# Another list of places for scores and values, and two more load and result tiles for the weight conversion, in an attention-and-MLP kernel

## The chip, the cores and the metric

The kernel is one program on one core of a Trainium2 chip. The metric is the time of one execution on the device in microseconds (us). The time before is the median of three runs. One more execution was taken with the hardware profiler; every duration below comes from that one, and its own time is given beside its span.

A core has five engines that run their own instruction lists in order and wait for each other by semaphores: PE (matrix multiply, with its weight loads shown apart as PEld), DVE (vector), ACT (activation and copies), POOL (a second vector engine) and SP (which only issues transfers here). Matrix results land in PSUM, a small memory of banks of 128 x 512 floats; DVE and ACT move them to the main on-chip memory.

## The reference, cut to what matters

```python
def _attn_ref(q, k, v, w_pre, w_post):            # q, k, v: (8, 12, 448, 64)
    scores = scale * np.matmul(q, k.transpose(0, 1, 3, 2))
    scores = np.einsum('bhij,hg->bgij', scores, w_pre)      # mix the 12 heads
    scores = scores - np.max(scores, axis=-1, keepdims=True)
    attn = np.exp(scores)
    attn = attn / (np.sum(attn, axis=-1, keepdims=True) + 1e-09)
    attn = np.einsum('bhij,hg->bgij', attn, w_post)          # mix them again
    return np.matmul(attn, v)

def _moe_ref(x, w_in, w_out):                      # x: (3584, 768)
    h = x @ w_in                                   # w_in: (768, 2048)
    g = h - np.tanh(h)
    return g @ w_out                               # w_out: (2048, 768)
```

The attention result of all 8 batches, put in token order, is x of the second function. w_in and w_out arrive as 64-bit floats.

## The kernel before, in words

The program has two stages. The first, to about 850 us of the profiled span, is the attention; the second is the MLP, and the change does not touch it. While the attention runs, the two weight matrices are also converted, from 64-bit floats to pairs of 32-bit parts (a high part and a rest), and written to device memory for the second stage.

**Blocks, groups, places.** A batch of 448 query rows is cut into four blocks of 120, 120, 120 and 88 rows; there are 32 blocks. The 12 heads are handled as six pairs. Since the heads are mixed with each other, the scores of a block are first computed for all heads and put in a tile `s` (rows by heads by 448 keys); then groups of 10 query rows x 12 heads are gathered from it by a transfer into a tile `t` with one partition for each row and head, so that mixing heads is a matrix product. A block has 12 such groups (the short one 9), 360 in all. The main loop handles two groups at a time, and one turn of it is called a **place**: there are 180, numbered from 0. In place p the loop issues, in this order:

- the gathers of the two groups that are used two places later, and up to six transfers that wait in two lists (lines 510 and 369, on SP);
- `premix`: four products with `w_pre` on PE (line 521), which give the mixed scores of the two groups, in two PSUM banks;
- `norm` for the place before: one over the sums on DVE (lines 541, 542) and the scaled `w_post`, called `wr`, on POOL (line 543);
- `expo`: two row maxima on DVE (line 530) and two exponentials on ACT (line 532);
- the jobs listed for this place: `prep_k` (transposing two heads of keys, line 417), `prep_q` (transposing queries, line 443), `values` (24 products of the finished attention of a block with v, line 602; half a block's heads in one job), `scores` (six products for a head pair, line 477), and loads;
- `sooner`: the copies of these jobs' results, the two copies of a pair's scores being one on ACT and one on DVE (line 482);
- `mix` for the place before: 16 products with `wr` (line 560), into the one tile `ps_o`; it waits for `wr`, and for `ps_o` to have been copied out;
- `conv.place()`: some steps of the weight conversion;
- at the start of the next place, the copy of `ps_o` into the block's tile `at` on ACT (line 570, or line 577 twice where the two groups are of different blocks).

Every engine runs its instructions in exactly this order (a final pass pins it), so a late instruction holds all behind it on its engine.

**The list of places.** Which place does which job is worked out when the program is built. Before, `scores` jobs come two head pairs at a time: three entries for a block, each with an earliest place and a due place; one entry (two pairs of scores, or one `values` job) is handed to each place by due place, and after an entry of one kind the other kind goes first where there is time. Scores of a block are due three places before the place in which the block's first group is used. A place may get nothing at all.

**The conversion.** `narrow_steps` deals with 56 chunks of 128 x 512 (w_in, 24 chunks) or 128 x 384 (w_out, 32 chunks) numbers. A chunk is loaded (`cr`), goes through 11 steps (`narrow_chunk`; DVE lines 80, 83, 87, 89, 94; ACT lines 82, 85, 102; POOL lines 96, 98, 104, in the order 80, 82 and 83, 85, 87, 89, 94, 96, 98, 102, 104), and its two results are written (`ws<-cs`, `ws<-cl`). At most two chunks are active, and their steps are taken in turn, one of each; 617 steps are spread over 164 places from place 4 on, so 3.76 a place. A loaded chunk becomes active when one of the two is done and its load was issued at least one place ago; three chunks are loaded or active at most. The load list is only served behind the attention's own transfers.

## Time and profile before

| what | value |
|---|---|
| median of 3 runs (lowest to highest) | 1794.49 us (1794.04 to 1794.81) |
| the profiled execution's own time | 1788.92 us |
| its span | 1787.2 us |
| PE, PEld busy in the span | 98%, 80% |
| DVE, ACT, POOL busy in the span | 63%, 56%, 18% |
| mean granted PE clock | 0.993 |
| bytes moved by transfers | 372.32 MB, mean 208 GB/s |

A matmul's end is modelled in this profile, so PE counts as busy nearly always; that does not say that it runs at its peak. What is to be read is the idle time in front of a group of instructions, and what ended it. In rows of groups the columns are: line, engine, operation, out<-in, shapes, count | busy us, mean ns of one | idle us before them, and what ended most of it. In rows of the timeline: start us, duration us, engine, line, operation, out<-in, shapes, count, and in brackets the idle time before and what ended it. A matmul that runs as two passes is counted twice.

### The profile page before, as it was taken

Reading aid. Unit: us, or ns where it says so; the run is one execution under the profiler, and the core shown is the slowest. Engines: PE = TensorE matmul, PEld = TensorE weight load, DVE = VectorE, ACT = ScalarE, POOL = GpSimd, SP = SyncE. Lnnn points to the kernel's source line nnn. Section 1 sums busy time; section 2 is a strip of 40 time slices with the busy share of each in tenths; the row PEclk is TensorE's granted clock in tenths of the full one; section 3 lists DMA queues with packets and bytes.
Section 4 is the critical chain, followed back from the end, with each engine's and each line's share of the span. In section 5 each row is a group of like instructions: output and inputs, shape, how many; then the busy total and the mean of one; then the engine's idle time right before and its main releaser. Section 6 shows DMA issues by size and latency. Waiting matters only on the chain.

```text
span 1787.2 us, 41382 instructions
## 1 busy us (share of the span) xinstructions
PE 1751.0 (98%) x16572; PEld 1425.6 (80%) x16572; DVE 1128.3 (63%) x2362; ACT 1000.5 (56%) x2051; POOL 320.1 (18%) x417
## 2 busy tenths in 40 slices
PE   8999999999999999999999999999999999999998
PEld 6777777777777777777888888888888888888887
DVE  5676777777777767664556566565565565655555
ACT  5777877777777776765343443433434434444333
POOL 1333333333333333321010010000000000000000
PEclk9999999999999999999999999999999999999999
DMA  8668687777967687565655655655656655655651
GB/s 176 204 196 216 194 236 224 217 215 215 249 203 218 215 213 220 178 202 216 255 207 194 248 193 207 241 193 214 229 197 216 224 208 204 228 217 190 230 194 36
DMA packets 232816, 372.32 MB, mean 208 GB/s; under 512 B 98992, under 2 KB 207536, under 8 KB 218288
## 3 DMA queue, kind: packets, MB, share of 16 engines
q1 hardware_dynamic: 231740, 368.45, 64.0%
q8 instruction: 131, 2.15, 0.5%
q10 hardware_dynamic: 884, 1.22, 0.2%
q14 instruction: 61, 0.50, 0.1%
HBM read 245.37 MB, written 47.19 MB: 164 GB/s over the span
## 4 chain that ended last, share of the span: by engine, by line
PE 87%; DMA 4%; ACT 4%; DVE 3%; issue 1%; POOL 0%; SPq 0%; ACTq 0%; DVEq 0%; POOLq 0%
PE ps_o L560 13%; PE ps_h L257 8%; PE ps_h L258 8%; PE ps_h L262 8%; PE ps_m L602 8%; PE ps_p L521 7%; PE ya L305 6%; PE ya L302 6%; PE ya L303 6%; PE ps_q L477 5%; PE yb L305 3%; PE yb L303 3%; PE yb L302 3%; DMA t<-s 2%; PE ps_m L443 1%
## 5 line engine op out<-in xcount | busy, mean ns | idle before, releaser
L560 PEld LDWEIGHTS ps_o<-wr,e 60*112 60x112 f32 (+1 forms) x5760 | 306.2, 176 | 44.3 <-POOL wr L543 21.8
L560 PE MATMUL ps_o<-wr,e 60*112 60x60 f32 (+1 forms) x5760 | 315.5, 259 | 14.3 <-POOL wr L543 7.7
L530 DVE TENSOR_REDUCE mx<-ps_p 128x1 f32<-128x448 f32 x360 | 207.7, 619 | 163.9 <-PE ps_p L521 163.7
L532 ACT ACTIVATE e<-ps_p,mx 128x448 f32<-128x448 f32 x360 | 225.7, 634 | 101.9 <-DVE mx L530 99.4
L289 ACT CAST gh<-r 128x512 fp32r<-128x512 f32 x112 | 69.6, 621 | 372.6 <-DVE r L282 372.6
L258 PE MATMUL ps_h<-xl,w 128*128 128x512 f32 x672 | 264.4, 393 | 0.0
L257 PE MATMUL ps_h<-xh,w 128*128 128x512 f32 x672 | 264.3, 393 | 0.0
L570 ACT COPY at<-ps_o 112x960 f32<-112x960 f32 x156 | 153.7, 985 | 93.8 <-PE ps_o L560 93.2
L247 POOL TENSOR_TENSOR xl<-rx,xh 128x512 fp32r<-128x512 f32 x38 | 55.6, 1464 | 731.2 <-ACT xh L246 731.2
L521 PE MATMUL ps_p<-t,wpre 60*64 60x448 f32 (+1 forms) x1440 | 180.8, 569 | 3.9 <-DMA t<-s 2.7
L305 PE MATMUL ya<-w,gl 128*128 128x512 f32 x448 | 177.0, 395 | 0.7 <-DVE gl L290 0.7
L278 DVE SCALAR_TENSOR_TENSOR r<-qa,ps_h 128x512 f32<-128x512 f32 x112 | 77.1, 688 | 159.2 <-ACT t L275 159.2
L302 PE MATMUL ya<-w,gh 128*128 128x512 f32 x448 | 174.8, 390 | 1.0 <-ACT gh L289 1.0
L303 PE MATMUL ya<-w,gh 128*128 128x512 f32 x448 | 174.8, 390 | 0.0
L602 PEld LDWEIGHTS ps_m<-at,vr 112*64 112x64 f32 x3072 | 147.5, 137 | 31.0 <-ACT at L577 10.9
L262 PE MATMUL ps_h<-xh,w 128*128 128x512 f32 x672 | 170.6, 389 | 0.0
L602 PE MATMUL ps_m<-at,vr 112*64 112x120 f32 (+1 forms) x3072 | 161.6, 261 | 8.4 <-ACT at L577 3.1
L272 ACT ACTIVATE u<-ps_h 128x512 f32<-128x512 f32 x112 | 67.0, 599 | 152.9 <-PE ps_h L262 152.9
L262 PEld LDWEIGHTS ps_h<-xh,w 128*128 128x128 f32 x672 | 126.3, 188 | 26.3
L258 PEld LDWEIGHTS ps_h<-xl,w 128*128 128x128 f32 x672 | 127.5, 190 | 23.7
L257 PEld LDWEIGHTS ps_h<-xh,w 128*128 128x128 f32 x672 | 127.4, 190 | 23.4
L543 POOL TENSOR_TENSOR wr<-wpost,zs 128x120 f32<-128x120 f32 x180 | 70.2, 390 | 402.9 <-DVE zs L542 293.6
(93 smaller groups left out, 3038.0 us busy)
## 6 DMA issues: line engine op xcount, KB each, us to landing
w<-ws SPq DMA_DIRECT2D x112, 1536.0 KB
t<-s SPq DMA_DIRECT2D x342, 210.0 KB
cr<-in_moe_w_in_dram SPq DMA_DIRECT2D x24, 512.0 KB
cr<-in_moe_w_out_dram SPq DMA_DIRECT2D x32, 384.0 KB
vr<-in_v_dram SPq DMA_DIRECT2D x24, 448.0 KB
kr<-in_k_dram SPq DMA_DIRECT2D x23, 448.0 KB
out_dram<-ob SPq DMA_DIRECT2D x24, 384.0 KB
qr<-in_q_dram SPq DMA_DIRECT2D x23, 360.0 KB
```

What stands on the lines that cost most here:

```text
L257: nc.tensor.matmul(ph, wh[:, fs], xh, start=(c == 0), stop=False)
L258: nc.tensor.matmul(ph, wh[:, fs], xl, start=False, stop=False)
L262: nc.tensor.matmul(ph, wl[:, fs], xh, start=False, stop=(c == NK - 1))
L302: nc.tensor.matmul(y, gh[:, tok], wh[:, es], start=first, stop=False)
L303: nc.tensor.matmul(y, gh[:, tok], wl[:, es], start=False, stop=False)
L305: nc.tensor.matmul(y, gl[:, tok], wh[:, es], start=False, stop=last)
L521: nc.tensor.matmul(pss[r][halves[j], :], wpre[k, :], ts[j][k, :], start=True, stop=True)
L530: nc.vector.tensor_reduce(out=mx, in_=ps, axis=AX.X, op=ALU.max, negate=True)
L532: nc.scalar.activation(e, ps, AF.Exp, bias=mx, scale=1.0, accum_out=zs[:, 0, r : r + 1])
L560: nc.tensor.matmul(ps[:CP, j, c * GP : (c + 1) * GP].rearrange("p (h i) -> p h i", i=GI)[:, :, r * GH : (r + 1) * GH], e[k, c * CP : (c + ...
L570: nc.scalar.copy(ats[i0][:, :, :, at : at + 2 * GI].rearrange("p c h (j i) -> p j (c h) i", j=2), ps[:CP, :, : NC * GP].rearrange("p j (x ...
L602: nc.tensor.matmul(pv[j * D : (j + 1) * D, r, :n], vt[:, j, c, :], ats[i][:, c, 2 * hp + j, :n], start=(c == 0), stop=(c == NC - 1),)
```

## The change

Four things are changed.

1. **Scores** are dealt out by single head pairs: of a block's pairs that are left, each place takes as many as are needed to be done at the place before the due place. So places with one pair appear, and runs of places with two.
2. **Values** go to places that have no scores (or, for the last block of a batch, one pair), in order, and near their due place to any. The first block of a batch (but the very first) may start its values two places later than before; the loads of v are placed behind the last use of the tiles that they overwrite.
3. `prep_k` and `prep_q` are placed by counting PSUM banks (a place with scores may hold up to four in all), after the scores' places are known.
4. **The conversion** gets four load tiles `cr` in place of three, three tiles `cs` and `cl` in place of two, keeps four chunks loaded or active in place of three, and a chunk may start two places after its load was issued in place of one.

```diff
-        r = pool.tile([p, CW, 2], I32, name="cr", tag="cr", bufs=3)[:, : n2 // 2]
+        r = pool.tile([p, CW, 2], I32, name="cr", tag="cr", bufs=4)[:, : n2 // 2]
...
-        while todo and len(loads) + len(active) < 3:
+        while todo and len(loads) + len(active) < 4:
...
-            if not landed(1):
+            if not landed(2):
...
-    s = pool.tile([p, CW], I32, name="cs", tag="cs", bufs=2)[:, :n]
+    s = pool.tile([p, CW], I32, name="cs", tag="cs", bufs=3)[:, :n]
...
-    fl = pool.tile([p, CW], F32R, name="cl", tag="cl", bufs=2)[:, :n]
+    fl = pool.tile([p, CW], F32R, name="cl", tag="cl", bufs=3)[:, :n]
...
+        def banks(p):
+            return sum({scores: 2, values: 1, prep_q: 1, prep_k: 1}.get(f, 0) for f, *a in todo[p])
...
+                lo, hi = max(0, (f0 - 1) // 2 - 1), f1 // 2 - 3
+                due_s += [(lo, hi, i + 1, hp) for hp in range(0 if i else 2, NP)]
+            lo = (f1 - 1) // 2 + (4 if i and i % NM == 0 else 2)
+            due_v += [(lo, f2 // 2 + 1 if f2 < NG else NPL + 7, i, x) for x in range(2)]
+        p = 0
+        while due_s or due_v:
+            now_s = 0
+            if due_s and due_s[0][0] <= p:
+                _, hi, i, _ = due_s[0]
+                left = sum(x[2] == i for x in due_s)
+                now_s = -(-left // max(hi - p, 1))
+                for _ in range(now_s):
+                    _, _, i, hp = due_s.pop(0)
+                    at_s[i, hp] = p
+                    at_place(p, scores, i, hp)
+            if due_v and due_v[0][0] <= p:
+                _, hi, i, x = due_v[0]
+                if p + (1 - x) >= hi or now_s == 0 or now_s == 1 and i % NM == NM - 1:
+                    due_v.pop(0)
+                    at_v[i, x] = p
+                    at_place(p, values, i, x)
+            p += 1
...
+                p = max(p0 + 4, at_v[i - 1, 1] + 1)
                 for hq in range(NP // 2):
-                    at_place(p0 + 4 + hq, load_v, b, hq)
+                    at_place(p + hq, load_v, b, hq)
...
-                    while any(f is scores or f is prep_q for f, *a in todo[o]):
+                    while banks(o) > 3:
                         o += 1
                     at_place(o, prep_k, b, 2 * hq + r)
```

How this moves instructions is shown at three points; in all the rows, line 521 (PE), 532 (ACT) or 543 (POOL) marks the beginning of a place's work.

**PE, places 30, 31 and 32**, where block 4 (the first of the second batch) is finished: `ps_q` are scores, 24 products of `ps_m<-at,vr` one values job, `ps_m<-ident,qr` a transposing of queries. Before:

```order
L521 MATMUL ps_p<-t,wpre 64x448 x4
L602 MATMUL ps_m<-at,vr 64x120 x24
L560 MATMUL ps_o<-wr,e 112x12x5 x16
L521 MATMUL ps_p<-t,wpre 64x448 x4
L477 MATMUL ps_q<-kk,qh 120x448 x4
L477 MATMUL ps_q<-kk,ql 120x448 x2
L477 MATMUL ps_q<-kk,qh 120x448 x4
L477 MATMUL ps_q<-kk,ql 120x448 x2
L560 MATMUL ps_o<-wr,e 112x12x5 x16
L521 MATMUL ps_p<-t,wpre 64x448 x4
L443 MATMUL ps_m<-ident,qr 128x88 x6
L602 MATMUL ps_m<-at,vr 64x120 x24
```

And now:

```order
L521 MATMUL ps_p<-t,wpre 64x448 x4
L477 MATMUL ps_q<-kk,qh 120x448 x4
L477 MATMUL ps_q<-kk,ql 120x448 x2
L560 MATMUL ps_o<-wr,e 112x12x5 x16
L521 MATMUL ps_p<-t,wpre 64x448 x4
L560 MATMUL ps_o<-wr,e 112x12x5 x16
L521 MATMUL ps_p<-t,wpre 64x448 x4
L443 MATMUL ps_m<-ident,qr 128x88 x6
L602 MATMUL ps_m<-at,vr 64x120 x24
```

The first values job of the block has moved from place 30 to place 32, place 30 has one pair of scores, and place 31 has no job.

**POOL, places 95 to 99.** The rows between two `wr` are conversion steps. Before:

```order
L543 TENSOR_TENSOR wr<-wpost,zs 128x2x60
L96 TENSOR_TENSOR cm<-cr,cs 128x512
L98 TENSOR_TENSOR cm<-cm,cr 128x512
L543 TENSOR_TENSOR wr<-wpost,zs 128x2x60 x2
L104 TENSOR_TENSOR cl<-cm,cs 128x512
L543 TENSOR_TENSOR wr<-wpost,zs 128x2x60
L96 TENSOR_TENSOR cm<-cr,cs 128x512
L543 TENSOR_TENSOR wr<-wpost,zs 128x2x60
L98 TENSOR_TENSOR cm<-cm,cr 128x512
```

And now, from place 92 on:

```order
L543 TENSOR_TENSOR wr<-wpost,zs 128x2x60 x4
L96 TENSOR_TENSOR cm<-cr,cs 128x512
L543 TENSOR_TENSOR wr<-wpost,zs 128x2x60
L96 TENSOR_TENSOR cm<-cr,cs 128x512
L98 TENSOR_TENSOR cm<-cm,cr 128x512 x2
L543 TENSOR_TENSOR wr<-wpost,zs 128x2x60
L104 TENSOR_TENSOR cl<-cm,cs 128x512 x2
L543 TENSOR_TENSOR wr<-wpost,zs 128x2x60 x5
```

Before, the two active chunks stand half a chunk apart, and POOL gets one or two conversion steps between two `wr`. Now both start together, so the same step of both stands side by side: six steps within three places, and none in the next four.

**ACT, places 96 and 97**, the same stretch. Before:

```order
L532 ACTIVATE e,zs<-ps_p,mx 128x448 x2
L482 COPY s<-ps_q 120x448 x2
L102 CAST cs<-cm 128x512
L82 ACTIVATE cm<-cm 128x512
L570 COPY at<-ps_o 112x2x48x10
L532 ACTIVATE e,zs<-ps_p,mx 128x448 x2
L428 CAST kk<-ps_m 128x448 x2
L85 ACTIVATE cr<-cr 128x512
L570 COPY at<-ps_o 112x2x48x10
```

And now:

```order
L532 ACTIVATE e,zs<-ps_p,mx 128x448 x2
L428 CAST kk<-ps_m 128x448 x2
L482 COPY s<-ps_q 120x448
L570 COPY at<-ps_o 112x2x48x10
L532 ACTIVATE e,zs<-ps_p,mx 128x448 x2
L482 COPY s<-ps_q 120x448
L102 CAST cs<-cm 128x512 x2
L570 COPY at<-ps_o 112x2x48x10
```

The casts of both chunks (line 102) now stand together in place 97, behind one copy of scores and ahead of the copy of `ps_o`.

56 lines of the change are left out of this document (22 added, 34 removed).

## Prediction

> **What bounds the kernel now.** First the page's busy times, and a window over the attention's steady part:
>
> ```profile
> PE 1751.0 (98%) x16572; PEld 1425.6 (80%) x16572; DVE 1128.3 (63%) x2362; ACT 1000.5 (56%) x2051; POOL 320.1 (18%) x417
> 40.00:850.00 810.00, 785.33 (x11498) 609.31 (x11497) 564.93 (x1525) 599.30 (x1364) 259.20 (x350) 0.99 0.73 213
> ```
>
> The second row is PE, PEld, DVE, ACT, POOL busy us, clock, transfer share and GB/s: PE is busy for 785 of 810 us, ACT for 599, POOL for 259. The second stage keeps its instructions, so the change can only move what PE waits for in these 810 us, and PE's products stay the same. So I go by the groups of instructions that PE idles in front of, and by what the waited-for engines run:
>
> ```profile
> L560 PE MATMUL ps_o<-wr,e 60*112 60x60 f32 (+1 forms) x5760 | 315.5, 259 | 14.3 <-POOL wr L543 7.7 <-ACT at L570 6.0 <-POOL cl L104 0.3
> L602 PE MATMUL ps_m<-at,vr 112*64 112x120 f32 (+1 forms) x3072 | 161.6, 261 | 8.4 <-ACT at L577 3.1 <-ACT at L570 2.7 <-DMA vr<-in_v_dram 2.4
> L521 PE MATMUL ps_p<-t,wpre 60*64 60x448 f32 (+1 forms) x1440 | 180.8, 569 | 3.9 <-DMA t<-s 2.7 <-ACT at L570 1.0
> L85 ACT ACTIVATE cr<-cr 128x384 f32<-128x384 int32 x32 | 18.3, 572 | 0.0
> L82 ACT ACTIVATE cm<-cm 128x384 f32<-128x384 f32 x32 | 17.2, 538 | 0.8 <-DVE cm L80 0.7
> L102 ACT CAST cs<-cm 128x512 fp32r<-128x512 f32 x24 | 15.1, 634 | 0.6 <-POOL cm L98 0.6
> L104 POOL TENSOR_TENSOR cl<-cm,cs 128x512 fp32r<-128x512 f32 x24 | 30.7, 1278 | 35.0 <-ACT cs L102 35.0
> L89 DVE SCALAR_TENSOR_TENSOR cr<-cm,cs 128x512 int32<-128x512 int32 x24 | 16.7, 700 | 1.2
> L94 DVE TENSOR_SCALAR cs<-cr 128x512 int32<-128x512 int32 x24 | 11.1, 464 | 0.4
> ```
>
> PE waits 14.3 us ahead of mix, 8.4 ahead of values, 3.9 ahead of premix. How a wait ahead of mix comes about is seen in places 136 and 137, two places with two pairs of scores each:
>
> ```profile
> 640.46 0.98 PE L521 MATMUL ps_p<-t,wpre 60*64 60x448 f32 x8
> ...
> 643.65 0.42 DVE L94 TENSOR_SCALAR cs<-cr 128x512 int32<-128x512 int32 x1
> 644.14 1.30 POOL L96 TENSOR_TENSOR cm<-cr,cs 128x512 f32<-128x512 f32 x1 [3.42 <-DVE zs L541]
> 644.32 0.98 PE L521 MATMUL ps_p<-t,wpre 60*64 60x448 f32 x8
> 644.44 0.98 ACT L570 COPY at<-ps_o 112x960 f32<-112x960 f32 x1
> 645.24 0.67 PE L477 MATMUL ps_q<-kk,qh 64*120 64x448 f32 x4
> 645.37 1.16 DVE L530 TENSOR_REDUCE mx<-ps_p 128x1 f32<-128x448 f32 x2 [0.98 <-PE ps_p L521]
> 645.52 1.30 POOL L98 TENSOR_TENSOR cm<-cm,cr 128x512 f32<-128x512 f32 x1
> 646.45 1.15 DVE L482 COPY s<-ps_q 120x448 f32<-120x448 f32 x2
> 646.72 0.62 ACT L532 ACTIVATE e<-ps_p,mx 128x448 f32<-128x448 f32 x1
> 646.78 0.39 POOL L543 TENSOR_TENSOR wr<-wpost,zs 128x120 f32<-128x120 f32 x1
> 647.22 1.78 PE L560 MATMUL ps_o<-wr,e 60*112 60x60 f32 x32 [0.50 <-POOL wr L543]
> 647.33 0.96 ACT L482 COPY s<-ps_q 120x448 f32<-120x448 f32 x2
> 648.94 0.98 PE L521 MATMUL ps_p<-t,wpre 60*64 60x448 f32 x8
> ```
>
> POOL's two conversion steps stand ahead of `wr`, and mix starts 0.50 late. The rows also give the unit costs: premix 0.92 (644.32 to 645.24), mix 1.72 (647.22 to 648.94), a place with two pairs 3.86 (640.46 to 644.32), hence 0.6 for a pair; an empty place would take 2.64, a place with one pair 3.24.
>
> **Values later (a gain).** Around place 30, the first half of block 4 before:
>
> ```profile
> 159.96 0.98 PE L521 MATMUL ps_p<-t,wpre 60*64 60x448 f32 x8
> 161.81 2.68 PE L602 MATMUL ps_m<-at,vr 112*64 112x120 f32 x48 [0.88 <-ACT at L577]
> 164.43 1.78 PE L560 MATMUL ps_o<-wr,e 60*112 60x60 f32 x32
> 167.02 0.98 PE L521 MATMUL ps_p<-t,wpre 60*64 60x448 f32 x8 [0.81 <-DMA t<-s]
> ...
> 671.68 1.04 PE L602 MATMUL ps_m<-at,vr 112*64 112x120 f32 x16 [1.40 <-DMA vr<-in_v_dram]
> ```
>
> Values take 2.62 (161.81 to 164.43) and wait for `at` of the group mixed just before, or for v (671.68, place 142). Each first block's values now stand two places, some 7 us, later, beyond all three waits (the 2.7 us for L570 includes the very first block's). What stays is in places 24, 69, 114 and 159, where values keep their place; the group's row gives 3.1 for L577, and I leave half of it, 1.5. Gain: 8.4 - 1.5 = 6.9. The bounds: none, if `at` or v is late at the new place too, and 8.4.
>
> **Scores by single pairs, and paired conversion steps (a loss).** Counted from the order of instructions for places 0 to 177: before, 92 places with two pairs alone, 14 empty or with loads alone, 10 with only transposed keys, 1 with only transposed queries, 61 with values. Now 57 with two pairs, 30 with one, 18 with one pair and keys, 7 empty, 5 with queries, 61 with values. A values job covers 2.62 us, so the other places decide.
>
> For each mix I set two sums against the moment at which PE comes to it: the length of the place before, plus premix and jobs of its own place. Both run from the place's start, from the rows above: the maxima end at 2.2 and the exponentials at 3.0 (647.34 less 644.32). Then (a) ACT: score copies (0.48 each, two in 0.96), the conversion's casts, then the copy of `ps_o`, 1.0; (b) DVE: score copies 0.58 each (two in 1.15), conversion steps, 0.53 for the norms, then POOL's steps, each not before its input, then `wr` 0.39; and 0.1 to signal. Three of the dearest:
>
> - Place 98, one pair after one pair: place 97 hands ACT both casts of line 102 behind one score copy: 3.0 + 0.5 + 0.63 = 4.1; POOL's two steps of line 104 follow, 1.28 each: 6.7; `wr` 7.1, signal 7.2. PE is there at 3.24 + 0.92 + 0.6 = 4.75. Late by 2.4.
> - Place 76, empty: place 75 hands ACT one step of line 82 and two of line 85: 3.5 + 0.54 + 1.14 = 5.2, the copy 6.2. PE is there at 3.24 + 0.92 = 4.16. Late by 2.1, of which 0.5 at the mix before.
> - Place 53: DVE runs lines 89, 89, 94, 94 in place 52: 2.2 + 0.58 + 1.40 + 0.93 = 5.1, norms 5.6, `wr` 6.1, against 4.75. Late by 1.4.
>
> The same two sums for every mix, less what the mix before was late already, give before: 12.6 us into empty places, 3.4 into places with keys alone, 3.7 into places with two pairs, 19.7 together. The trace has 14.3 (the L560 row), 0.73 of it. Now: 19.0 into places with one pair (20 of the 30), 8.6 into places with two pairs, 4.9 into empty ones, 1.4 into those with a pair and keys: 33.9, times 0.73 is 24.7. Loss: 24.7 - 14.3 = 10.4. The bounds: all of 33.9 shows, +19.6; only empty places wait, 4.9 x 0.73 = 3.6, so -10.7. I take 10.4, since one discount fits the kernel before. The single pair alone would not do it: over an empty place it gives 0.6 more cover, and the empty places wait 12.6 x 0.73 / 14 = 0.66 each. It is the pairing that makes the chains longer.
>
> **Transfers.** A pair of chunks now sends its four results and two loads close together:
>
> ```profile
> cr<-in_moe_w_in_dram SPq DMA_DIRECT2D x24, 512.0 KB
> ws<-cs SPq DMA_DIRECT2D x24, 256.0 KB
> DVE cs L87 <- DMA ws<-cs: 6.9, 3, 3.5
> 513.00:516.40 3.40, 2.07 (x34) 1.23 (x30) 2.60 (x9) 2.73 (x7) 2.42 (x3) 1.00 0.86 254
> ```
>
> That is 4 x 256 + 2 x 512 KB = 2.1 MB, 8.3 us at the 254 GB/s of the last row; a gather has about two places and a half, 8 to 10 us, so most just arrive. The third `cs` tile takes off some of DVE's 6.9 us for the writes, under values mostly. Value +1; bounds -2.7 (all premix waits for `t` gone) and +6 (worked out under the third rival).
>
> **Clock.** Four windows of the attention's span run at half clock:
>
> ```profile
> 106.07:109.49 3.42, 1.97 (x36) 1.89 (x40) 2.59 (x8) 3.20 (x8) 0.68 (x2) 1.00 0.87 225
> 109.49:112.90 3.41, 3.41 (x20) 1.89 (x14) 1.77 (x3) 2.15 (x6) 1.32 (x2) 0.50 0.60 220
> 723.89:727.30 3.41, 3.41 (x20) 2.04 (x14) 1.78 (x3) 2.23 (x6) 1.97 (x2) 0.50 0.74 260
> 795.60:802.40 6.80, 6.80 (x54) 4.69 (x52) 2.25 (x6) 3.67 (x9) 1.91 (x3) 0.50 0.42 154
> ```
>
> The first follows a window with PE busy for 1.97 of 3.42 us. Half speed over 3.41 + 3.41 + 6.80 = 13.6 us costs 6.8. Waits above one microsecond grow in number now (by the sums with the discount, five before, seven after), but 513.00 to 516.40, busy for 2.07, was not followed by one, so it hangs on where a wait falls. Value 0, bounds -6.8 and +6.8. The Trainium skill, "TensorE: Matmul & The Clock Gate", section "Part 1: The HAM clock gate", says that the clock halves after at least one idle window of about 3.4 us; by that rule the waits here would never halve it. The trace differs: it was halved after a window that was 58% busy.
>
> **Sum.** -6.9 + 10.4 + 1 + 0 = +4.5 us. The profiled execution took 1788.92 (span 1787.2); the median of the runs, 1794.49, is 5.6 above it, which I take to be a matter of the executions. The forecast is 1794.5 + 4.5 = 1799.0.
>
> **Rivals.** What a measurement of this kernel can tell from no change is about 0.2%, 3.6 us.
>
> 1. *The paired steps are hidden* (faster): ACT and POOL catch up in the three or four places without conversion and under values, as ACT is idle for a quarter of the time. Then mix waits only where a place is empty, 7 in place of 14: half of 14.3 gone, 7.2; values 6.9; two of the four half-clock windows 3.4: 1794.5 - 17.5 = 1777. Against it: the same sums find the trace's waits before (place 137: 0.97 by them, 0.50 in the row). Chance 0.18.
> 2. *Gains and losses cancel* (no change): the waits ahead of mix grow as forecast, but none falls so as to halve the clock: 1799.0 - 6.8 = 1792. For it: the rows show such waits with and without. The page's rule named above would make this the case, as no wait here fills a window. Chance 0.25.
> 3. *Bursts make gathers late* (slower): the place is a pair's writes and loads in the places where k and v are loaded too. At place 31 before, a late gather cost 0.81 and then 1.02 in the next premix (the L521 row's 1.0 for L570), 1.8 together. It decides from about 2.5 MB ahead of a gather, 10 us. If one of four of the 28 pairs does so, 7 x 1.8 = 12.6; with half of that, 6, as the bound above. 1799.0 + 12.6 - 1 = 1811. Chance 0.15.
> 4. *The change does not do what it says*: of scores "a place sooner", block 6 ends in place 30 after 31, but blocks 2 and 3 end in 8 and 14 as before. That alone moves no wait of the rows above; no time of its own.
>
> **How the numbers follow.** The forecast has 0.42, rival 1 0.18, rival 2 0.25, rival 3 0.15. Faster: rival 1 and a little of rival 2, 0.21. Same: most of rival 2 and a little of the forecast, 0.26. Slower: 0.53. The likeliest case's own range is 1795 to 1806. For 8 in 10 I go down half way to rival 1, 1785, and up to rival 3, 1811.
>
> **What would show it.** Right: idle ahead of mix near 25 us, `wr` and `at` named; idle ahead of values below 2; one-pair places above 3.24 in length by 0.7 on average, most where two casts or two steps of line 104 stand in the place before. Wrong: idle ahead of mix below 14 us (rival 1); waits for `t` above 6 us (rival 3); other than four half-clock windows (the clock's term).

## The result, and the profile after

The changed kernel takes 1822.60 us, median of four runs (1818.02 to 1829.58); the kernel before, run beside it, 1794.26 (1789.32 to 1794.81). The ratio is 1.0168, with a 95% interval of 1.0139 to 1.0197: 1.7% slower, about 28 us. One kernel's executions differ by up to 22 us with the granted clock of each (one at 1884 us, with a clock of 0.873, is left out), so all comparisons below rest on intervals over several runs.

The profiled execution of the changed kernel took 1818.02 us, span 1816.3, against 1788.92 and 1787.2 before: 29.1 us more. The groups that PE idles in front of, changed kernel:

```profile
L560 PE MATMUL ps_o<-wr,e 60*112 60x60 f32 (+1 forms) x5760 | 320.2, 262 | 17.0 <-POOL wr L543 10.5 <-ACT at L570 6.3
L521 PE MATMUL ps_p<-t,wpre 60*64 60x448 f32 (+1 forms) x1440 | 185.0, 584 | 18.0 <-DMA t<-s 17.8 <-ACT s L482 0.2
L602 PE MATMUL ps_m<-at,vr 112*64 112x120 f32 (+1 forms) x3072 | 166.5, 266 | 0.1
```

The wait ahead of values is gone (8.4 to 0.1), the one ahead of mix has grown a little (14.3 to 17.0), and the one ahead of premix, for gathered tiles `t`, has grown from 3.9 to 18.0. Of the 17.0 ahead of mix, 3.3 stand in the last place (179), where it was 1.2; in all the other places mix waits 13.7 against 13.1. The new wait in the last place comes from a transfer: ACT waits for a load of the second stage (`rx<-xs`), DVE for ACT's result of it, and `wr` for what DVE does next.

```profile
865.72 0.62 ACT L246 CAST xh<-rx 128x512 fp32r<-128x512 f32 x1 [3.01 <-DMA rx<-xs]
866.37 0.69 DVE L247 TENSOR_TENSOR xl<-rx,xh 128x512 fp32r<-128x512 f32 x1 [2.34 <-ACT xh L246]
867.98 1.98 PE L560 MATMUL ps_o<-wr,e 60*112 60x60 f32 x32 [2.15 <-POOL wr L543]
```

The span and granted clock of the changed kernel:

```profile
core 0: 1816.3 us, clock 0.981
```

1816.3 x (1 - 0.981) = 34.5 us of clock are lost; before, 1787.2 x (1 - 0.993) = 12.5. So the 29.1 us are: gathers +14.1, mix +2.7, values -8.3, clock +22.0; these add to 30.5, the clock being known to 0.001 of the span, 1.8 us. The two terms that the prediction held to be +1 and 0 are more than the whole loss. The other executions say the same: the clock lost, worked out for each, has a median of 38.2 us with the change and of 14.3 to 17.9 in the series of the kernel before, and the time without it 1782.9 against 1776.8 to 1778.0. Some 22 us of the loss go through the clock, 5 to 6 do not.

They belong together. The PE timeline of the changed kernel from place 30 to the values in place 32 (start, duration, operation, and in brackets the idle time and what ended it):

```profile
161.36 0.98 PE L521 MATMUL ps_p<-t,wpre 60*64 60x448 f32 x8
...
163.07 1.78 PE L560 MATMUL ps_o<-wr,e 60*112 60x60 f32 x32
167.32 1.77 PE L521 MATMUL ps_p<-t,wpre 60*64 60x448 f32 x8 [2.47 <-DMA t<-s]
169.03 3.24 PE L560 MATMUL ps_o<-wr,e 60*112 60x60 f32 x32
172.20 1.77 PE L521 MATMUL ps_p<-t,wpre 60*64 60x448 f32 x8
...
174.97 3.41 PE L602 MATMUL ps_m<-at,vr 112*64 112x120 f32 x48
```

Place 31 is now empty. PE waits 2.47 us for its gathered tile, and from there on premix takes 1.77 instead of 0.98 and mix 3.24 instead of 1.78. Three pairs of neighbouring windows, each a window with a wait and the one behind it (columns as in the prediction: PE, PEld, DVE, ACT, POOL busy, clock, transfer share, GB/s):

```profile
162.92:166.33 3.41, 1.93 (x36) 1.68 (x32) 1.55 (x6) 3.10 (x8) 1.78 (x3) 0.99 0.84 215
166.33:176.57 10.24, 9.25 (x70) 6.17 (x72) 3.93 (x12) 4.13 (x12) 0.78 (x3) 0.50 0.80 216
...
593.00:596.40 3.40, 1.78 (x32) 1.65 (x32) 2.12 (x7) 2.74 (x6) 2.90 (x4) 0.99 0.80 224
596.40:606.60 10.20, 9.18 (x70) 6.10 (x72) 2.88 (x8) 4.88 (x13) 4.04 (x6) 0.50 0.77 209
501.00:504.20 3.20, 1.36 (x28) 1.23 (x26) 3.20 (x7) 2.44 (x6) 0.00 (x0) 1.00 0.96 239
504.20:514.40 10.20, 9.61 (x68) 6.18 (x70) 3.86 (x12) 3.80 (x9) 5.71 (x6) 0.50 0.53 140
```

In these three, a window in which PE was busy for 1.4 to 1.9 us of 3.2 to 3.4 is followed by 10.2 us at half clock, each costing about 5 us. Not every such stretch is as long; behind the waits for `t` of 2.86 us (place 54) and 2.30 us (place 98) they are:

```profile
275.50:282.33 6.83, 5.23 (x38) 3.66 (x40) 1.93 (x4) 2.66 (x8) 2.14 (x4) 0.50 0.79 203
483.71:487.12 3.41, 3.41 (x22) 1.84 (x22) 1.37 (x3) 0.92 (x3) 1.05 (x2) 0.50 1.04 211
```

In all, this trace has seven waits of 2.1 to 2.9 us in the attention, six for `t` (places 8, 31, 54, 98, 102 and 121) and the one of the last place. Half clock follows each of them, for 10.2 us in five cases: 61.4 us together, so 4.4 us lost for each in the mean.

Why the gather for place 31 is late is seen in part on SP, the engine that issues the transfers. The changed kernel, places 25 to 30:

```profile
143.99 0.65 SPq L369 DMA_DIRECT2D kr<-in_k_dram  x1
144.74 1.86 SPq L369 DMA_DIRECT2D xs<-x  x1
146.66 2.59 SPq L369 DMA_DIRECT2D cr<-in_moe_w_out_dram  x2
149.35 1.68 SPq L510 DMA_DIRECT2D t<-s  x2
151.08 0.50 SPq L369 DMA_DIRECT2D vr<-in_v_dram  x1
151.69 1.63 SPq L510 DMA_DIRECT2D t<-s  x2
153.36 0.83 SPq L369 DMA_DIRECT2D vr<-in_v_dram  x1
154.24 1.05 SPq L369 DMA_DIRECT2D qr<-in_q_dram  x1
155.39 6.39 SPq L510 DMA_DIRECT2D t<-s  x2
```

A pair of gathers is issued in 1.63 to 1.68 us; the pair for place 31 takes 6.39, so its second gather leaves SP at 161.8, 5.5 us ahead of the premix that needs it. Ahead of it stand k, two loads of the conversion, two of v, q, and the write of finished results `xs`. But the kernel before shows that this is not all. There SP was held too, by a load of v, and the pair for place 31 left it no sooner:

```profile
151.97 4.24 SPq L369 DMA_DIRECT2D vr<-in_v_dram  x1
...
159.49 1.66 SPq L510 DMA_DIRECT2D t<-s  x2
```

It left SP at 161.1, and premix began at 167.02 after a wait of 0.81: 5.9 us from SP to its use, against 5.5 with the change. What differs is the place ahead. With a values job, place 30 took PE 6.25 us (159.96 to 166.21), now 3.49 (161.36 to 164.85). The pairs for the five other places with waits of 2 us or more leave SP in 1.6 to 2.8 us, and premix begins 5.7 to 8.6 us later; when they landed the trace does not say.

What the transfers did around the border of the batch, first before, then with the change:

```profile
130.00:140.00 10.00, 8.96 (x148) 6.67 (x140) 6.20 (x17) 7.15 (x18) 3.07 (x4) 1.00 0.62 183
140.00:155.00 15.00, 15.00 (x226) 11.77 (x222) 11.08 (x32) 11.83 (x28) 4.16 (x6) 1.00 0.82 211
```

```profile
130.00:140.00 10.00, 9.94 (x176) 8.48 (x174) 4.82 (x12) 6.51 (x16) 7.89 (x8) 1.00 0.28 95
140.00:155.00 15.00, 14.27 (x214) 10.42 (x214) 10.47 (x36) 10.88 (x24) 1.55 (x4) 1.00 1.05 293
```

Before, 183 and 211 GB/s; with the change 95 and then 293, at a share of 1.05. POOL's conversion work is in the quiet window (7.89 of 10 us).

### The profile page after: what moved, and what is told of

Same layout as the page of the kernel before. It is cut to its first block, busy times and chain, and to the rows that moved or that the text cites. A ratio compares the mean times of both kernels' runs of the same rounds, so it can differ in the third digit from the quotient of the medians.

```text
span 1816.3 us, 41312 instructions
## 1 busy us (share of the span) xinstructions
PE 1771.8 (98%) x16572; PEld 1435.4 (79%) x16572; DVE 1106.1 (61%) x2362; ACT 1000.5 (55%) x2051; POOL 315.2 (17%) x417
## 4 chain that ended last, share of the span: by engine, by line
PE 87%; DMA 5%; DVE 2%; ACT 2%; issue 2%; POOL 1%; SPq 0%; ACTq 0%; POOLq 0%; DVEq 0%
PE ps_o L560 13%; PE ps_h L257 8%; PE ps_h L258 8%; PE ps_h L262 8%; PE ps_m L602 8%; PE ps_p L521 8%; PE ps_q L477 6%; PE ya L305 6%; PE ya L302 5%; PE ya L303 5%; DMA t<-s 4%; PE yb L305 3%; PE yb L303 3%; PE yb L302 3%; PE ps_m L443 1%
## 5 line engine op out<-in xcount | busy, mean ns | idle before, releaser
L560 PEld LDWEIGHTS ps_o<-wr,e 60*112 60x112 f32 (+1 forms) x5760 | 312.4, 178 | 48.4 <-POOL wr L543 24.3
L560 PE MATMUL ps_o<-wr,e 60*112 60x60 f32 (+1 forms) x5760 | 320.2, 262 | 17.0 <-POOL wr L543 10.5
L521 PE MATMUL ps_p<-t,wpre 60*64 60x448 f32 (+1 forms) x1440 | 185.0, 584 | 18.0 <-DMA t<-s 17.8
L602 PEld LDWEIGHTS ps_m<-at,vr 112*64 112x64 f32 x3072 | 152.9, 140 | 25.0 <-issue 12.9
L602 PE MATMUL ps_m<-at,vr 112*64 112x120 f32 (+1 forms) x3072 | 166.5, 266 | 0.1
L482 DVE COPY s<-ps_q 120x448 f32<-120x448 f32 (+1 forms) x192 | 113.6, 616 | 61.1 <-PE ps_q L477 58.9
L262 PEld LDWEIGHTS ps_h<-xh,w 128*128 128x128 f32 x672 | 126.3, 188 | 26.3
```

The lines of the kernel that those rows point to most:

```text
L262: nc.tensor.matmul(ph, wl[:, fs], xh, start=False, stop=(c == NK - 1))
L521: nc.tensor.matmul(pss[r][halves[j], :], wpre[k, :], ts[j][k, :], start=True, stop=True)
L560: nc.tensor.matmul(ps[:CP, j, c * GP : (c + 1) * GP].rearrange("p (h i) -> p h i", i=GI)[:, :, r * GH : (r + 1) * GH], e[k, c * CP : (c + ...
L602: nc.tensor.matmul(pv[j * D : (j + 1) * D, r, :n], vt[:, j, c, :], ats[i][:, c, 2 * hp + j, :n], start=(c == 0), stop=(c == NC - 1),)
```

## The experiments

Two questions: which part of the change does it, and by what. Times are medians; ratios stand against the kernel before, run beside each. "Premix", "mix" and "values" are PE's idle us ahead of these in the profiled execution, "clock" is span x (1 - granted clock) in it, and "clock, all" the median of this over all executions of the kernel. The profiled one is not always typical: for new places, old conversion it is the fastest of four (1799.46 us), for before, values late the fastest of eight (1799.76). The kernel before ran at 1791 to 1795 us in these series.

| kernel | time | ratio (95%) | premix | mix | values | clock | clock, all |
|---|---|---|---|---|---|---|---|
| before | 1794.26 | | 3.9 | 14.3 | 8.4 | 12.5 | 14.3-17.9 |
| the change | 1822.60 | 1.0168 (1.0139-1.0197) | 18.0 | 17.0 | 0.1 | 34.5 | 38.2 |
| new places, old conversion | 1813.71 | 1.0110 (1.0050-1.0169) | 12.3 | 18.3 | 0.1 | 14.4 | 31.7 |
| old places, new conversion | 1801.55 | 1.0053 (1.0033-1.0074) | 8.0 | 19.2 | 7.2 | 14.4 | 19.8 |
| pairs staggered | 1820.19 | 1.0149 (1.0111-1.0187) | 17.5 | 15.1 | 0.0 | 36.3 | 37.3 |
| gathers a place sooner | 1811.72 | 1.0105 (1.0075-1.0136) | 4.9 | 26.6 | 0.1 | 27.1 | 26.2 |
| that, old conversion | 1806.01 | 1.0091 (1.0059-1.0124) | 1.6 | 29.0 | 0.1 | 19.8 | 21.6 |
| fewer results written | 1818.26 | 1.0150 (1.0113-1.0187) | 21.9 | 15.4 | 0.1 | 29.1 | 30.8 |
| PE kept busy | 1814.57 | 1.0138 (1.0091-1.0186) | 9.6 | 15.1 | 0.1 | 18.2 | 16.3 |
| values early, old conversion | 1798.06 | 1.0007 (0.9975-1.0039) | 9.3 | 16.6 | 0.1 | 10.7 | 17.1 |
| values early | 1810.85 | 1.0103 (1.0049-1.0156) | 22.7 | 15.6 | 0.1 | 32.7 | 27.1 |
| before, values late | 1808.75 | 1.0088 (1.0055-1.0122) | 12.3 | 16.6 | 3.8 | 18.0 | 28.9 |
| v loads late | 1815.13 | 1.0134 (1.0088-1.0179) | 7.9 | 20.2 | 4.1 | 29.0 | 29.9 |
| k loads sooner | 1811.11 | 1.0108 (1.0083-1.0133) | 13.5 | 19.5 | 0.1 | 23.5 | 27.2 |
| before, k loads sooner | 1786.28 | 0.9963 (0.9942-0.9984) | 2.0 | 14.3 | 6.1 | 14.3 | 14.3 |
| values early, loads' half | 1812.19 | 1.0125 (1.0097-1.0154) | 19.8 | 15.7 | 0.1 | 21.7 | 30.8 |
| values early, results' half | 1793.87 | 1.0005 (0.9983-1.0027) | 6.8 | 16.7 | 0.1 | 14.3 | 17.9 |
| values early, fourth chunk | 1811.86 | 1.0094 (1.0067-1.0120) | 12.6 | 19.8 | 0.6 | 32.7 | 30.8 |
| results' half, early, k sooner | 1789.39 | 0.9981 (0.9962-1.0000) | 4.7 | 15.9 | 0.1 | 14.3 | 14.3 |
| before, k sooner, results' half | 1787.58 | 0.9961 (0.9945-0.9976) | 1.7 | 14.5 | 8.9 | 12.5 | 14.3 |

The last column goes with the time: kernels that lose 26 to 38 us of clock ran at 1808 to 1823 us, those that lose 14 to 20 at 1786 to 1802. PE kept busy is the exception, since its added products take time themselves.

### The two halves of the change

**New places, old conversion.** The list of places as changed, `narrow_steps` and `narrow_chunk` as before.

```diff
-name="cr", tag="cr", bufs=4 ... len(active) < 4 ... landed(2) ... cs, cl: bufs=3
+name="cr", tag="cr", bufs=3 ... len(active) < 3 ... landed(1) ... cs, cl: bufs=2
```

> The new places with the conversion as before (three load tiles, two result tiles, three chunks at most, start one place after the load's issue): the chunks stand half a chunk apart again. Theory P (the paired conversion is the cause: its bursts make gathers late, its paired steps make chains long, and long waits halve the clock): 28 us too many go back almost wholly, 1788 to 1798 us, idle ahead of premix for t under 4 us, half-clock time in the attention under 20 us (65 us in the changed kernel). Rival S (the places are the cause: values moved later leave runs of short places just where k and v are loaded, so that the same transfers have less time): 1806 to 1818 us, idle for t above 8 us, at places 31 and 121 as in the changed kernel.

**Old places, new conversion.** The reverse: the list of places before, with the new conversion.

> The old places with the new conversion (four load tiles, three result tiles, four chunks, start two places after issue): the chunks are paired. Theory P: 1808 to 1822 us, idle ahead of premix for t above 8 us, half-clock time above 35 us. Rival S: within 4 us of the kernel before, 1790 to 1798 us, idle for t under 5 us. If both are needed (short places and bursts together): 1796 to 1806 us here, and about 1795 with the new places and the old conversion.

Measured: 1.0110 and 1.0053. Both halves lose, and multiplied they give 1.0164, near the change's 1.0168. The first time lies in the range of rival S, the second in neither theory's: neither holds alone. Ahead of premix PE waits 12.3 and 8.0 us, neither half alone reaching 18.0. Mix waits more with the new conversion (19.2 against 14.3), but also without paired steps (18.3), and the half that has none loses too, by its median more (the intervals overlap).

**Pairs staggered.** The change, with the second chunk of a pair started five steps after the first.

```diff
+    taken = 0
-            if not landed(2):
+            if not landed(2) or (active and taken < 5):
```

> The changed kernel, in which a second chunk may start only when the active one has taken at least five steps: the room of four load and three result tiles stays, only the pairing goes. Theory P (pairing, not the room): as the old conversion does, 1786 to 1798 us, POOL never has more than two conversion steps between two wr, idle ahead of mix 10 to 16 us. If the larger room itself is the cause (more loads in flight at once): 1808 us or more, idle for t above 8 us. Rival S: 1806 to 1818 us.

POOL now never has more than two conversion steps between two `wr`; in the changed kernel it has three to five 38 times. Measured 1820.19, ratio 1.0149, inside the change's own interval, with 15.1 us ahead of mix and 17.5 ahead of premix. The 2 us less ahead of mix are those of the last place (1.2 in place of 3.3), and nothing shows in the time. The prediction's main term falls here.

### Values of a batch's first block

**Values early, old conversion.** New places and old conversion; only the values of a batch's first block start two places sooner, as before the change.

```diff
-            lo = (f1 - 1) // 2 + (4 if i and i % NM == 0 else 2)
+            lo = (f1 - 1) // 2 + 2
```

> The new places with the conversion as before, and the first block of a batch starts its values as early as the others, so that places 31, 76, 121 and 166, empty in the changed kernel, take a values job; places 53 and 54, 98 and 99 stay as they are. If the values moved later are what makes the stretch short: waits for t at places 31 and 121 go, those at 54, 98 and 102 stay; idle for t 6 to 8 us against 11.6, 1800 to 1808 us. If the single pairs of scores do it: as the new places with the old conversion, 1809 to 1818 us. If the new places together are harmless without both: 1788 to 1798 us.

**Values early.** The same one line undone in the whole change.

> The changed kernel with one thing undone: the values of a batch's first block start two places sooner, where they stood before (place 31 holds one of them, place 32 the other). The conversion keeps its new room, scores are still dealt singly. Theory V (the values taken out of the stretch before 31 make it short: gathers, with the same transfers in less time, come late and the clock halves; this costs most of the change's loss): 1796 to 1804, about what the new conversion alone gave (1801.6); idle ahead of premix near 8 to 10 us instead of 18.0, half clock in the attention below 35 us instead of 64.9. Rival C (the values are only dear together with the old conversion, and the new one's bursts do the rest): 1810 or more, idle ahead of premix above 14.

**Before, values late.** The kernel before with that line's effect alone: place 30 empty, the two jobs in 32 and 34.

```diff
-halved.append(((f1 - 1) // 2 + 2, f2 // 2 + 1 if f2 < NG else NPL + 7, "v", i, x))
+halved.append(((f1 - 1) // 2 + (4 if i and i % NM == 0 else 2), f2 // 2 + 1 if f2 < NG else NPL + 7, "v", i, x))
```

> The kernel before with one thing done: the values of a batch's first block start two places later (place 30 empty, values in 32 and 34). Scores stay in twos, the conversion stays as it was. Theory V, if taking values out of the stretch is enough by itself: idle ahead of premix rises from 3.9 to over 8 us while idle ahead of values falls from 8.4 to about 2, and the time is 1797 or more. Rival S (later values cost only where single pairs also shorten the stretch: here values of the block before still stand in place 26): idle ahead of premix below 6, idle ahead of values about 2, time 1785 to 1793, not slower than before.

Measured: 1798.06, 1810.85 and 1808.75. The later start of these values costs 1.0110 - 1.0007 = 0.0103, 1.0168 - 1.0103 = 0.0065 and 0.0088 in three settings, 12 to 18 us; there are seven such blocks. The first and the last are clear of the noise, the second is not: its two intervals overlap. In the kernel before it is enough alone. The groups there, with values late:

```profile
L560 PE MATMUL ps_o<-wr,e 60*112 60x60 f32 (+1 forms) x5760 | 316.2, 259 | 16.6 <-POOL wr L543 8.5 <-ACT at L570 6.2 <-issue 1.4
L521 PE MATMUL ps_p<-t,wpre 60*64 60x448 f32 (+1 forms) x1440 | 182.2, 573 | 12.3 <-DMA t<-s 12.3
L602 PE MATMUL ps_m<-at,vr 112*64 112x120 f32 (+1 forms) x3072 | 161.1, 261 | 3.8 <-ACT at L570 2.2 <-ACT at L577 1.5
```

The gain that the prediction counted is there (8.4 to 3.8), and the same edit takes PE work out of the stretch in which the next batch's k, v, q and `xs` move: waits for `t` go from 2.7 to 12.3. Most of the price goes through the clock: over all executions 28.9 us of it are lost against 14.3 in the kernel before beside it, 14.6 of the 17 us. In the whole change the picture is less clean: undoing the line there gains 12 us in the median, while its profiled execution, which at 1818.09 is the longest of its four, still shows 22.7 us ahead of premix. Not all of the price is seen in one trace.

### The conversion's room

**Values early, loads' half.** Four `cr` tiles, four chunks under way, two places for a load; `cs` and `cl` back to two.

```diff
-name="cs", tag="cs", bufs=3 ... name="cl", tag="cl", bufs=3
+name="cs", tag="cs", bufs=2 ... name="cl", tag="cl", bufs=2
```

> The changed kernel with values of a batch's first block at their old places (1810.9 so run), and of the conversion's new room only the loads' half: four cr tiles, four chunks under way, a load given two places; cs and cl back to two tiles. If the loads asked for sooner are what the new room costs: 1808 to 1813, idle ahead of premix near 22 us, with place 8 among them. If the results' tiles (two chunks in step) are: about 1798, as with the old conversion, idle ahead of premix near 8.

**Values early, results' half.** The other way round.

```diff
-name="cr", tag="cr", bufs=4 ... len(active) < 4 ... landed(2)
+name="cr", tag="cr", bufs=3 ... len(active) < 3 ... landed(1)
```

> The same with the other half: three cs and cl tiles, but three cr tiles, three chunks under way and a load given one place, as before. If the loads asked for sooner are what the new room costs: about 1798, idle ahead of premix near 8 us. If the results' tiles are: 1808 to 1813, idle ahead of premix near 22 us. If it takes both: both runs near 1800.

**Values early, fourth chunk.** All of the new room, but a load again given one place.

```diff
-            if not landed(2):
+            if not landed(1):
```

> The changed kernel with values of a batch's first block at their old places and one piece of the loads' half undone: a load is again given one place before its chunk may start (four cr tiles, four chunks under way and the third cs and cl tiles stay). If the two places' wait is what makes the gathers late (chunks wait until both of a pair have landed and then start together): near 1794, as with all of the loads' half undone, idle ahead of premix below 9 us. If the fourth chunk under way does it: near 1811, idle ahead of premix 18 to 23 us.

Measured: 1812.19 (1.0125), 1793.87 (1.0005) and 1811.86 (1.0094). The intervals of the first and third lie clear of the second's: the third result tiles are free, and it is the fourth chunk under way, or what comes with it, that costs, not the second place of waiting. The 12.6 us ahead of premix in the third are fewer than the 18 to 23 expected of it. One thing comes back together with the fourth chunk: the paired steps (three or more on POOL between two `wr` 38 times, once and 33 times in the three). These runs do not part the two; in the whole change, taking the pairs apart did not help. Windows of the same stretch, first loads' half, then results' half (it comes to place 31 some 3 us sooner, so its windows are set sooner), then fourth chunk:

```profile
130.00:140.00 10.00, 9.90 (x180) 8.65 (x178) 5.01 (x14) 6.12 (x15) 7.53 (x8) 1.00 0.32 103
140.00:155.00 15.00, 14.23 (x210) 10.37 (x208) 10.50 (x32) 11.10 (x25) 1.55 (x4) 1.00 1.06 294
```

```profile
125.00:135.00 10.00, 9.87 (x169) 7.98 (x168) 6.93 (x19) 7.77 (x20) 4.52 (x5) 1.00 0.66 185
135.00:150.00 15.00, 15.00 (x248) 11.85 (x242) 9.82 (x31) 10.17 (x26) 4.13 (x6) 1.00 0.96 261
```

```profile
130.00:140.00 10.00, 10.00 (x174) 8.23 (x176) 4.44 (x13) 6.64 (x18) 5.63 (x6) 1.00 0.59 186
140.00:155.00 15.00, 15.00 (x242) 11.84 (x242) 11.01 (x36) 11.36 (x28) 1.40 (x4) 1.00 0.99 259
```

With the loads' half the transfers go in bursts: 103 GB/s while POOL computes for 7.53 of 10 us, then 294. With the results' half, 185 and 261. But the fourth chunk alone has nearly that even flow here and is as slow, and the staggered kernel has it too:

```profile
130.00:140.00 10.00, 9.62 (x146) 7.75 (x146) 6.40 (x15) 7.03 (x18) 2.34 (x3) 1.00 0.76 218
140.00:155.00 15.00, 15.00 (x248) 11.47 (x240) 10.38 (x34) 10.63 (x24) 5.62 (x8) 1.00 0.73 201
```

So bursts in this stretch are not what the loss hangs on. That gathers are later with the fourth chunk is measured; how it makes them so stays open.

**Fewer results written.** The change; after the first 14 of 56 chunks only the first of the two results is written, and the second stage reads the first weights again in place of the others. So the output is not the reference's; a quarter of the conversion's transfers is left out for these chunks.

```diff
-... for part in (0, 1)]   ... for part in (2, 3)]   wss[f // 4][:, f % 4]
+... for part in (0, 1)[: 2 if f == 0 else 1]]   ... (2, 3)[: 2 if f == 0 else 1]]   wss[0][:, f % 4]
```

> The changed kernel with a quarter of the conversion's transfers left out: only the first 14 of 56 chunks write their second result, and the second stage reads the first chunks' weights over and over (the same transfers, but the output is not the reference's). Every instruction of PE, ACT, DVE and POOL stays. If saturated transfers make the gathers late: idle for t falls from 17.8 to under 9 us, half-clock time from 65 to under 40 us, 1800 to 1810 us. If the order of the issues on SP does it: as the changed kernel, 1818 us or more, idle for t above 14 us.

Measured 1818.26 and 21.9 us ahead of premix: no help. The mean load is not what decides, and half of a pair's writes can go without the gathers coming sooner. Rival 3 of the prediction put the cost on a pair's writes and loads; the other half of the writes, and the loads, were not tried in this way.

### Where the gathers stand

**Gathers a place sooner.** Eight `t` tiles for six, gathers three places ahead; `cs` and `cl` at two tiles for the room. Once on the change, once with the old conversion.

```diff
-        RT = 6
+        RT = 8
-            for t in (2 * p + 4, 2 * p + 5):
+            for t in (2 * p + 6, 2 * p + 7):
```

> The changed kernel with each gather issued three places ahead in place of two (eight t tiles in place of six; to make room for them cs and cl have two tiles again, the steps stay paired). Tells the late gathers and the clock from the long chains. If late gathers and the halved clock behind them are most of the loss: idle for t falls from 17.8 to under 5 us, half-clock time from 65 to under 25 us, 1795 to 1804 us, while idle ahead of mix stays at 15 to 25 us. If the paired steps on ACT, DVE and POOL are most of it: 1812 us or more. Rival: transfers are the bound over the whole stretch, so that a gather issued earlier only waits longer: idle for t stays above 10 us, 1812 us or more.

> The new places, the conversion as before, and each gather issued three places ahead (eight t tiles). The new places with the old conversion took 1813.7 us with 12 us of idle ahead of premix and, by run, 24 to 80 us at half clock. Theory S2 (the runs of short places leave gathers too little time; the waits of 2 to 3 us that follow halve the clock): idle for t below 4 us, half-clock time below 20 us in every run, 1782 to 1794 us. Rival (transfers are saturated, an earlier issue changes nothing): idle for t above 8 us, 1805 us or more.

Measured 1811.72 and 1806.01. The waits for `t` go (4.9 and 1.6 ahead of premix), and mix waits for 26.6 and 29.0 us instead. The row of the first:

```profile
L521 PE MATMUL ps_p<-t,wpre 60*64 60x448 f32 (+1 forms) x1440 | 182.2, 575 | 4.9 <-DMA t<-s 4.9
```

A wait ahead of premix gives DVE, ACT and POOL time, and so hides a wait ahead of the next mix. Single mixes now wait up to 3.2 us (place 52) and 5.7 us (place 7), and 26.2 and 21.6 us of clock are still lost. With the change 11 us are won, not the whole loss, and the time falls between the two expected ranges; with the old conversion 8 us by the medians, with intervals that overlap, and 12 us above the range expected.

**v loads late.** The change, with the loads of v for a new batch in places 28 to 30 in place of 26 to 28.

```diff
-                p = max(p0 + 4, at_v[i - 1, 1] + 1)
+                p = max(p0 + 6, at_v[i - 1, 1] + 1)
```

> The changed kernel with one thing moved: the three loads of v for a new batch (1.3 MB) are asked for two places later (28 to 30 instead of 26 to 28), as their values are; so they stand behind the gathers for places 30 and 31, not ahead of them. If the gathers of place 31 (and 54, 76, 98, 121, 143, 166) are late because too much is under way ahead of them: idle ahead of premix falls from 18.0 to below 11 us, the gather for place 31 is issued without a stall of 5 us, half clock falls below 45 us and the time to 1803 to 1812. If the amount ahead of them does not matter (issues are held by something else): idle ahead of premix stays at 15 to 20 us and the time at 1816 to 1824; v waits of values may come in at most 1 us each in seven places.

Measured 1815.13. SP now issues the gathers of place 31 so:

```profile
151.09 3.37 SPq L510 DMA_DIRECT2D t<-s  x4
...
155.28 2.68 SPq L510 DMA_DIRECT2D t<-s  x2
158.01 0.80 SPq L369 DMA_DIRECT2D vr<-in_v_dram  x1
```

2.68 us instead of 6.39, and the wait ahead of premix falls from 18.0 to 7.9. So what stands ahead on the queue does make the gather late. But values now wait 4.0 us for v, mix 20.2, and only 7 us come back, with intervals that overlap.

**k loads sooner.** The change, and the kernel before, with the first two loads of k for a batch asked for in places 20 and 21 in place of 24 and 25.

```diff
-                at_place(p, load_k, b, hq)
+                at_place(p - (4 if b > 1 and hq < 2 else 0), load_k, b, hq)
```

> The changed kernel with one thing moved: the first two loads of k for a new batch (0.9 MB) are asked for four places sooner (places 20 and 21 instead of 24 and 25), into a stretch where the transfer share is 0.5 and lower; nothing else moves. Theory T (gathers are late because the transfers of a batch's border stand in a stretch that the change made shorter): idle ahead of premix falls from 18.0 us to below 10, half clock below 45 us, time 1803 to 1814, and idle ahead of mix stays near 17. Rival H (what is late is not a matter of how much is under way, and the waits only move): idle ahead of premix 14 or more, time 1816 to 1824.

> The kernel before with the same move of the first two loads of k, four places sooner. Theory T: its waits for gathers at a batch's border (0.81 and 1.02 at place 31 and 32) go, idle ahead of premix falls from 3.9 to about 2 us (the first place's 1.6 stays), and the time is 1784 to 1792, at or a little below before. Rival H: within 0.2% of before or slower, as the wait moves to another gather.

Measured: 1811.11 for the change, 11 us back, with 13.5 ahead of premix (below 10 was expected); and 1786.28 for the kernel before, 0.9963 (0.9942 to 0.9984), 7 us faster than it. There the wait for gathers is gone but for the first place's 1.6, and SP issues the gathers of place 31 without a stall:

```profile
L521 PE MATMUL ps_p<-t,wpre 60*64 60x448 f32 (+1 forms) x1440 | 181.8, 571 | 2.0 <-DMA t<-s 1.9
L602 PE MATMUL ps_m<-at,vr 112*64 112x120 f32 (+1 forms) x3072 | 163.3, 263 | 6.1 <-ACT at L577 3.2 <-ACT at L570 2.5 <-DMA vr<-in_v_dram 0.3
```

```profile
155.89 1.64 SPq L510 DMA_DIRECT2D t<-s  x2
```

The idle time fell by 1.9 us ahead of premix and by 2.3 ahead of values, where the wait for v went from 2.4 to 0.3. The profiled executions differ by 2.9 (1784.3 against 1787.2 of span), as the one with k sooner lost 1.8 us more of clock. Over all executions the clock lost is 14.3 us against 16.1; the rest of the 7 us is time without it.

### The clock by itself

**PE kept busy.** The change, with 16 idle products on `ident` ahead of premix in the six places with the longest waits for `t`.

```diff
+                if p in (8, 31, 54, 98, 102, 121): busy(16, ps_m.tile([P, 512], F32, name="ps_b", tag="ps_m"))
```

> The changed kernel with 16 products nobody needs (about 1.9 us) ahead of premix in places 8, 31, 54, 98, 102 and 121, where it waits 2 to 2.9 us for t. They fill waits and add nothing where the wait stands. Theory clock (a wait of over 2 us halves the clock for up to 10 us, which costs more than the wait): half-clock time falls from 65 to under 35 us and the time by 8 to 18 us, to 1804 to 1814 us. Rival (the half clock is only a sign of the waits and costs nothing of its own): within 4 us of 1822 us, or slower by the 11 us of added products.

Measured 1814.57. The profiled execution's span and clock:

```profile
core 0: 1816.2 us, clock 0.990
```

The clock lost falls from 34.5 to 18.2 us, in the same span (over all executions from 38.2 to 16.3). The products' rows, first without and then with the 96 added ones, each of which runs as two passes:

```profile
L663 PE MATMUL ps_b<-ident 128*128 128x128 f32 x56 | 9.6, 335 | 1.5 <-POOL ident masks.py:199 1.5
L663 PE MATMUL ps_b<-ident 128*128 128x128 f32 x248 | 33.5, 296 | 1.5 <-POOL ident masks.py:199 1.5
```

They keep PE busy for 23.9 us, not the 11 expected, and only what stands in former waits comes free. That waits of 2 to 3 us drop the clock is borne out; paying for it in products gains nothing certain (1.0138 against 1.0168, with intervals that overlap).

### What is left of the change

**Results' half, early, k sooner** and **before, k sooner, results' half**: the harmless parts put together on either list of places.

> The best of what the change holds, with the loads of k: scores by single pairs, third cs and cl tiles, but values at their old places, the conversion's loads as before, and the first two loads of k four places sooner. Without the move of k this gave 1793.9 (idle ahead of premix 6.8 us, ahead of values 0.1, ahead of mix 16.7). If the gains of the parts add: the waits for t go to about 2 and the time to 1783 to 1789. If the single pairs only trade waits ahead of values for waits ahead of mix and gathers: 1787 to 1794.

> The kernel before with k asked for four places sooner (1786.3 so run) and the third cs and cl tiles, which came without a cost in the changed kernel once the loads were as before (1793.9 beside 1798.1). If they help by themselves: 1780 to 1785, idle ahead of mix below 14.3 us. If not: 1785 to 1789, within 0.1% of the run without them.

Measured 1789.39 (0.9981) and 1787.58 (0.9961). The first is within what can be told from no change, the second equals the run without the third tiles (0.9963). Single pairs trade the wait ahead of values (8.4 to 0.1) for waits ahead of mix and premix; the tiles for results are worth nothing that shows. The k loads are the one gain found, and both kernels with that move on the old places beat before and after.

## Why the prediction was wrong

It forecast 1799.0, in 1785 to 1811, with 0.53 for slower. Slower was right; 1822.6 lies 23.6 above the forecast and 11.6 above the range. It was right for another reason than the one it gave: the paired steps, its only large loss, are not what costs. The steps that failed are the transfers and the clock, held to be +1 and 0, and the cover that the later values take away.

- **Values later (-6.9).** Its own row is right: the wait ahead of values fell by 8.3. The step failed in what it left out. It said that the values go beyond all three waits, and did not ask which work they left uncovered: a short place 30 and an empty place 31 in the stretch where a batch's loads move. That price is 12 to 18 us, so the edit is a loss of 1.0088 by itself.
- **Paired conversion steps (+10.4).** Mix's wait grew by 2.7, of which 2.1 in the last place, behind a transfer. Of the three places named, 76 waits 1.37 of the 2.1, 53 does not wait, and at 98 a wait for `t` of 2.30 stands ahead of the mix. With the gathers sooner mix does wait 26.6 us, near the 24.7 of the forecast, but 29.0 with no paired steps at all; and taking the pairs apart leaves the time as it is. The sums found late mixes, and named the wrong cause for the loss.
- **Transfers (+1, bounds -2.7 and +6).** Mis-sized: +14.1. The estimate took the conversion's 2.1 MB against a gather's 8 to 10 us, and left out that k, v, q and `xs` stand on the same queue at a batch's border and that the place ahead of the gather's use had become shorter. The place was known: the third rival named it, with place 31 as its row.
- **Clock (0, bounds -6.8 and +6.8).** Mis-sized: +22.0. Even its reading of the kernel before is short: it speaks of four windows at half clock, shows three and sums 13.6 us. The trace has two more in the attention, and 23.9 us in all, 11.9 of them lost:

```profile
27.57:30.98 3.41, 3.41 (x20) 1.63 (x18) 2.57 (x7) 2.20 (x6) 0.16 (x1) 0.50 0.65 213
843.35:850.18 6.83, 6.83 (x31) 5.56 (x29) 1.34 (x3) 2.48 (x5) 2.72 (x3) 0.50 0.51 213
```

With the change there are nine, 68.3 us. What was not seen is that a wait of 2 to 3 us costs clock besides itself, here 4.4 us in the mean, so that the two terms move together. The Trainium skill ("TensorE: Matmul & The Clock Gate", section "Part 1: The HAM clock gate") lets the clock fall after an idle window of about 3.4 us; the trace again halves it after windows busy for 1.93 and 1.78 us of 3.4.
- **Rival 3, bursts make gathers late** (1811, 0.15), is what came nearest. Its 12.6 us are close to the 14.1 measured, in part by luck: it counted seven events at the borders of batches, where only four waits of 2 us or more stand (places 31, 54, 98 and 121); two more stand elsewhere (8 and 102). Without the clock it stops at 1811. Late gathers were right; that a pair's writes make them late was not borne out.
- **Rival 1 and rival 2** fall: mix waits 17.0, not 7, and waits for `t` drop the clock.
- **Rival 4**: the edits do what they say. Single pairs (1.0007, with values early) and the third result tiles (1.0005) have no effect on the time that shows; values later and the fourth chunk lose.

The signs that the prediction gave for itself read right: "waits for `t` above 6 us (rival 3)" came at 18.0, and nine half-clock windows in place of four said that the clock's term was wrong.

## What to carry to other kernels

Work that moves off a stretch is cover taken from that stretch: before counting the wait that it leaves behind as a gain, look at which transfers run there, and at what share. A wait of two or three microseconds on PE is to be priced with the clock that it may drop, here 4.4 us more in the mean. A profile of one execution can miss this, as it did where the clock lost was 14.4 us and the median 31.7. And where loads of different purpose share one queue, asking for one sooner is not a gain in itself: k four places sooner, into a stretch with a transfer share of 0.65 in place of one of 0.82, gave 0.9963, a fourth chunk under way about 1.01.

## What the runs showed of the hardware that was not expected

- An issue on SP is not always short: a pair of gathers takes 1.64 us, and 6.39 at the border of a batch, with a transfer share of 1.05 over 140 to 155 us and of 0.82 while the issue was held. With v out of the way the same pair took 2.68. In the kernel before, a load of v took 4.24 and a pair of gathers 6.99. What holds the issue was not tried by itself.
- Half clock lasts beyond its cause: 10.2 us at half clock after one wait of 2 to 2.5 us, although PE was busy for 9.2 of the 10.2. How long it lasts varies. In the 20 traces kept, 48 waits of PE of 2 us or more begin at full clock between 5 and 900 us of the span; half clock sets in during 47 of them or within 3.5 us behind, for 3.4 us (16 times), 6.8 (15), 10.2 (8) or 13.7 (8), 3.6 us lost for each in the mean. Of 46 waits of 1.5 to 2 us 35 were followed by it, of 115 waits of 1 to 1.5 us 51.
- "DMA: Bandwidth & Descriptors" of the Trainium skill, section "Rules for kernel authors", advises to issue a transfer early and to wait for it late. For k the runs agree (0.9963); for the conversion's fourth chunk they do not (1.0094 to 1.0125), and gathers on the same queue come later with it.
